# One transformer block on one core: the split of the third attention tile of each later group moves to the end of its slot

## Chip, cores and metric

The kernel runs on one core of a Trainium2 chip. A core has five engines with instruction queues of their own: TensorE (PE, matrix products), VectorE (DVE), ScalarE (ACT), GpSimd (POOL) and SyncE (SP, which here only issues DMAs). Each queue is worked off in the order in which it was written; an instruction that waits for another engine holds all that stand behind it in its own queue. The metric is the device time of one execution in microseconds (us): 510.4 us before, the median of three runs (510.28 to 510.7).

## The reference

A pre-norm transformer block on 2048 positions of width 512: attention in which each position sees itself and seven earlier positions, two apart (32 heads of width 16), and an MLP of width 1792 with a squared ReLU.

```python
def _A_ref(x, wqkv, wo):                       # H = 32, Dh = 16
    W, dil = 8, 2
    q, k, v = ...                              # of x @ wqkv
    idx = pos[:, None] - (jnp.arange(W) * dil)[None, :]
    logits = einsum("bhsd,bhswd->bhsw", q, k[idx]) * Dh ** -0.5
    attn = softmax(where(idx >= 0, logits, -1e9))
    o = einsum("bhsw,bhswd->bhsd", attn, v[idx])
    return o.reshape(B, S, D) @ wo

h  = x + _A_ref(layernorm(x), wqkv, wo)
r  = maximum(layernorm(h) @ w1 + b1, 0)
h2 = h + (r * r) @ w2 + b2
```

## The kernel before, in words

**Tiles and passes.** The positions are cut into 16 tiles of 128 (`t` = 0 to 15), four of which make a group. A first part computes q, k and v of all tiles. Then a loop over `u` = 0, 1, 2 (called the first, second and third pass below) runs the MLP of group `u` on TensorE while the tiles `4(u+1)` to `4(u+1)+3` of the next group are brought through attention, output projection and normalisation; `i` = 0 to 3 is a tile's place in its group. The last group has a loop of its own. TensorE's products are float32 made of three rounded products (high by high, low by high, high by low), so each operand is split into a high part (`hi`, ScalarE, L152) and a low part (`lo`, a subtraction on VectorE or GpSimd, L155).

**A pass.** It has 17 slots `p`. In slot `p`, TensorE gets the first MLP product of hidden block `p` (`mlp1`, L228, 12 matmuls into a bank `mm`) and the second product of block `p` - 3 (`mlp2`, L895, 12 matmuls into four banks `acc`). A bank `mm` is read out one slot later by ScalarE (`hidden`: L871, L872, then the high part `rh` at L152); its low part `rl` is a subtraction on GpSimd (L155).

**Attention** is a stream of steps that runs beside this and keeps VectorE and GpSimd busy: products of q and k (L339, `dots`; q lies in a bank `qp` that ScalarE fills, L268), their sums (L373), maximum and subtraction (L390, L392), the exponential on ScalarE (L396), the weighted values (L350, `weigh`), whose eight terms GpSimd adds up into the result tile `o` (L407, three instructions). `pump` issues as many of these steps as fit the slot by a running estimate of VectorE's and TensorE's time.

**From attention to the MLP.** A finished tile of `o` must be transposed. For the tiles 4 to 15 (`OV`) this is done by DMA in steps: `o_split` first issues attention steps until the tile is complete, then copies its two 16-bit planes apart (ScalarE, L616, `pl<-o`); `turn_dma` (SyncE, L620) transposes the planes; `o_join` two slots later joins them (ScalarE, L625), makes the high part (L152, `oh` or `ohl`) and, on VectorE, the low part (L155, `ol` or `ohl`). `wo_product` projects it (TensorE, L228, `wo`), `h_add` adds the residual and takes statistics (VectorE, L661, L163, L164, or ScalarE, L182 to L184), GpSimd turns these into a scale (L169 to L172 or L188 to L191, `rs`), `h_norm` applies it (ScalarE, L196, `hn`), and the result is transposed for the MLP by DMA (tiles in `HV`) or by TensorE (L201).

**What sets the order.** Chores are put into one of three lists for a slot: `at` (run first), `midway` and `after`. `end_slot` runs the `at` list, then the attention stream, then `midway`, then `after`:

```python
    def end_slot(pe):
        now["pe"] += pe
        run(due)
        pump()
        run(amid)
        run(late)
        now["slot"] += 1
```

The table `todo` says in which slot of a pass each step of a tile is put into which list. The third tile of a group (`i` = `RI` = 2: tiles 6, 10 and 14) has its split in slot 10 of the first two passes and slot 9 of the third. There the `at` list also holds the read-out of the bank `mm`, and the `after` list ends with the normalisation `h_norm` of an earlier tile.

Of the kernel before, what the change touches and what calls it, by code (L numbers as in the profile page):

```python
# [20 lines left out]
RI = 2  # L21
# [37 lines left out]
def block_kernel(ctx, tc, x, wqkv, wo, w1, b1, w2, b2, out):  # L59
# [53 lines left out]
    def at(delta, fn, *a):  # L113
        due.setdefault(now["slot"] + delta, []).append((fn, a))
# [7 lines left out]
# [8 lines that stand above are left out]
    def run(chores):  # L130
        todo = chores.get(now["slot"], [])
        while todo:
            fn, a = todo.pop(0)
            fn(*a)

    def dve(t):
        now["dve"] += t
# [739 lines left out]
    def mlp1(u, f):  # L877
        ps = turn["mm"].tile("mm")
        fs = slice(f * P, (f + 1) * P)
        mm3(ps, lambda k: w1_h[:, k, fs], lambda k: w1_l[:, k, fs],  # L880
            lambda k: hh[k // 2][:, k % 2], lambda k: hl[k // 2][:, k % 2])
        at(1, hidden, u, f, ps)

    def mlp2(u, f, acc, js, first=False, last=False, mid=None):

        rh, rl = hid[u, f]
        terms = [(rh, w2_h, j) for j in js] + [(rh, w2_l, j) for j in js]
        if len(js) > 1:
            terms += [(rl, w2_h, j) for j in js]
        else:  # L890
            terms.insert(1, (rl, w2_h, js[0]))
        for n, (l, w, j) in enumerate(terms):
            if mid and n == len(terms) // 2:
                mid()
            nc.tensor.matmul(acc[j], l[:, j * P:(j + 1) * P], w[f],  # L895
                             start=(first and n < len(js)),
                             stop=(last and n >= len(terms) - len(js)))
# [79 lines left out]
    for n in range(16):  # L977
        gp, t = divmod(n, 4)
# [72 lines left out]
    def load_w2(f):  # L1051
        raws[f] = row("raw2")
        nc.sync.dma_start(raws[f], w2[f * P:(f + 1) * P, :])
# [36 lines left out]
    for u in range(R - 1):  # L1090
        now["sub"] = u
        first, end = u == 0, False
        fs = list(range(FB)) if first else [*sorted(place), 12, 13]
        fs += [f for f in range(12) if f not in fs and (u < 2 or f not in ENDS)]
        fs += ENDS if u == 2 else []
        need = [] if first else [f for f in fs if f < 12 and f not in place]
        acc = [psum.tile([P, D], F32, name="acc", tag=tag) for tag in ("acc0", "acc1", "tr0", "tr1")]
        js = range(R)


        todo, halves = {}, {}
        for i in js:
            t = R * (u + 1) + i
            if not end:
                a = i // 2 if u == 2 else 0
                o0 = OP[i] - a - (2 if i >= RI and t in OV else 0)
                if t in OV:
                    turned = [(o0, at, 0, o_split, t), (o0, at if i >= RI else after, i // RI, turn_dma, ("o", t)),
                              (o0 + 2, at, 0, o_join, t)]
                else:  # L1110
                    turned = [(o0, o_T, t)]
                if t in HV:
                    h0 = 11 + i
                    turned += [(h0, midway, 0, h_split, t), (h0, after, 0, turn_dma, ("h", t)),
                               (h0 + 2, at, 0, turn_join, ("h", t))]
                for p, *what in ((LH[i] - a, at, 0, load_h, t), *turned,
                                 (WP[i] - a, wo_product, t, (0, 1, 2 + 3 * a, 3 + 3 * a))):
                    todo.setdefault(p, []).append(what)
                p, h = (HP[i], i % 2) if u < 2 else HL[i]
                if t in HV:  # L1120
                    todo.setdefault(p, []).append((at, 0, h_parts, t))
                else:
                    (todo, halves)[h].setdefault(p, []).append((h_T, t))
            todo.setdefault(UP[i], []).append((at, 0, unspill, R * u + i))
        if u == 2:
            for p, *what in ((12, at, 0, t_load, 0), (12, at, 0, t_load, 1), (13, after, 0, t_sums, 0),
                             (13, after, 0, t_sums, 1), (13, at, 1, t_split, 0),
                             (14, after, 0, t_split, 1)):
                todo.setdefault(p, []).append(what)

        def half(p):
            run(due)
            for fn, *a in halves[p]:
                fn(*a)

        for p in range(FB + LAG):
            more = 0.0
            if p == FB:
                run(due)
                dve(HOLD)  # L1140
            if u < 2 and p == FB - 2:
                dve(HOLD)
            for fn, *a in sorted(todo.get(p, []), key=lambda x: x[0] is wo_product):
                fn(*a)
                more += 2.73 if fn is wo_product else 0.0
            if p < FB:
                mlp1(u, fs[p])
                more += 2.73
                if first:
                    at(0, split_w2, p)  # L1150
                    if p + 1 < FB:
                        load_w2(p + 1)
            q = p - LAG
            if q >= 0:
                f = fs[q]
                mlp2(u, f, acc, js, q == 0, q == FB - 1,
                     (lambda: half(p)) if p in halves else None)
                more += 2.74
                if f < 12 and (need or first and p < FB - LAG):
                    free.append(place.pop(f))  # L1160
                    if need:
                        at(1, fetch, need.pop(0))
            end_slot(more)
        for i in js:
            at(u // 2, finish, R * u + i, acc[i])
# [83 lines left out]
```

## Time and profile before

| | before |
|---|---|
| median of three runs | 510.4 us |
| the profiled execution's own time | 510.82 us |
| its span, first to last instruction | 509.0 us |
| TensorE busy | 98 % of the span |
| VectorE, ScalarE, GpSimd busy | 75 %, 60 %, 70 % |
| HBM traffic over the span | 190 GB/s |
| first, second, third pass of the loop over `u` (TensorE) | about 163 to 252, 253 to 342, 343 to 430 us |

The profile is of one execution. In its rows a time is the start in us from the beginning of the span, the next number a duration in us, then come the engine, the source line, the operation, the tile written and the tile read, and a count of instructions merged into the row. A bracket at the end gives how long the engine was idle before the row and who released it. Ends of matmuls are modelled, so four matmuls are shown with a duration of 1.07 us but the next four start 0.91 us after them; only starts are compared below.

### The profile page before, as it was taken

What the parts mean: (1) busy time and instruction counts of PE and PEld (TensorE: products, weight loads), DVE (VectorE), ACT (ScalarE), POOL (GpSimd) and SP (SyncE); (2) the same over time, 40 slices, a digit from 0 to 9 for tenths busy, and PEclk for the clock granted to TensorE, in tenths of its full rate; (3) what the DMA queues carried; (4) which work ended last, traced back from release to release, by engine and by line L of the source; (5) the groups of instructions that cost most, each with busy time, mean ns of one, the idle gap of its engine ahead of it and who ended that gap; (6) DMA issues with size and microseconds to landing.
All of it is one profiled execution on the core that took longest, in us unless ns stands there. A gap on an engine that the chain in (4) does not pass through costs nothing.

```text
span 509.0 us, 7539 instructions
## 1 busy us (share of the span) xinstructions
PE 498.7 (98%) x2422; PEld 420.7 (83%) x2422; DVE 380.8 (75%) x512; ACT 304.7 (60%) x558; POOL 357.2 (70%) x434
## 2 busy tenths in 40 slices
PE   8999999999999999999999999989999999999997
PEld 7999778888888888887788888768888888998986
DVE  6469899999989799979879997898973137832233
ACT  4625677768346757386564566754556947566541
POOL 5714689986685899969777876976897465685610
PEclk9999999999999999999999999999999999999999
DMA  8577899989798898669676874967662372444212
GB/s 265 162 238 204 229 300 297 262 271 317 219 220 254 277 283 253 231 176 245 193 249 199 215 195 130 263 221 231 210 160 67 102 217 82 166 127 142 64 42 82
DMA packets 109359, 102.61 MB, mean 202 GB/s; under 512 B 29448, under 2 KB 77832, under 8 KB 109320
## 3 DMA queue, kind: packets, MB, share of 16 engines
q1 hardware_dynamic: 108376, 101.61, 68.0%
q10 hardware_dynamic: 944, 0.52, 0.3%
q8 instruction: 19, 0.31, 0.3%
q14 instruction: 20, 0.16, 0.1%
HBM read 72.65 MB, written 24.25 MB: 190 GB/s over the span
## 4 chain that ended last, share of the span: by engine, by line
PE 41%; POOL 5%; ACT 4%; DMA 3%; DVE 1%; issue 1%; SPq 0%; POOLq 0%; DVEq 0%; ACTq 0%
PE acc L895 19%; PE mm L228 12%; PE mm L818 6%; PE wo L228 3%; POOL pr L407 2%; DMA o<-pl 1%; DMA hn<-pl 1%; POOL h L674 1%; DMA h<-h_d 1%; ACT pl L625 1%; ACT pl L616 1%; ACT hn L196 1%; DVE pr L350 0%; POOL o L407 0%; PE tr L201 0%
## 5 line engine op out<-in xcount | busy, mean ns | idle before, releaser
L407 POOL TENSOR_TENSOR pr<-pr 128x512 f32<-128x512 f32 (+1 forms) x128 | 133.7, 1044 | 34.6 <-DVE pr L350 29.1
L228 PE MATMUL mm<-big_l,w_h 128*128 128x512 f32 x336 | 88.5, 390 | 1.6 <-DVE big_l L155 0.9
L350 DVE TENSOR_TENSOR pr<-ex,v 128x1024 f32<-128x1024 f32 x64 | 78.1, 1221 | 13.1 <-POOL o L407 8.1
L339 DVE TENSOR_TENSOR pr<-qp,k 128x1024 f32<-128x1024 f32 x64 | 76.8, 1200 | 8.8 <-ACT qp L268 6.9
L373 DVE TENSOR_REDUCE ex<-pr 128x64 f32<-128x1024 f32 x64 | 78.5, 1226 | 1.9
L228 PEld LDWEIGHTS mm<-big_l,w_h 128*128 128x128 f32 x336 | 62.9, 188 | 15.4 <-issue 1.3
L155 POOL TENSOR_TENSOR rl<-r,rh 128x512 fp32r<-128x512 f32 x42 | 55.5, 1322 | 20.2 <-ACT rh L152 20.2
L228 PE MATMUL mm<-big_l,xh 128*128 128x512 f32 (+1 forms) x208 | 55.8, 378 | 0.0
L228 PE MATMUL mm<-big_h,xh 128*128 128x512 f32 (+1 forms) x208 | 53.9, 380 | 1.3 <-ACT xh L152 1.0
L228 PE MATMUL mm<-big_h,xl 128*128 128x512 f32 (+1 forms) x208 | 52.7, 375 | 0.7 <-DVE xl L155 0.7
L895 PE MATMUL acc<-big_l,rh 128*128 128x512 f32 x190 | 52.2, 390 | 0.0
L895 PE MATMUL acc<-big_h,rh 128*128 128x512 f32 x190 | 52.1, 391 | 0.0
L895 PE MATMUL acc<-big_h,rl 128*128 128x512 f32 x190 | 51.7, 389 | 0.0
L228 PEld LDWEIGHTS mm<-big_h,xh 128*128 128x128 f32 x208 | 37.6, 188 | 8.9 <-ACT xh L152 2.6
L228 PE MATMUL mm<-big_l,w_l 128*128 128x512 f32 x168 | 44.9, 389 | 0.0
L228 PEld LDWEIGHTS mm<-big_h,xl 128*128 128x128 f32 x208 | 38.2, 188 | 6.9 <-DVE xl L155 1.1
L871 ACT ACTIVATE r<-mm,b_sb 128x512 f32<-128x512 f32 x42 | 28.7, 684 | 22.5 <-PE mm L228 20.7
L895 PEld LDWEIGHTS acc<-big_h,rl 128*128 128x128 f32 x190 | 35.7, 188 | 7.4
L895 PEld LDWEIGHTS acc<-big_l,rh 128*128 128x128 f32 x190 | 35.5, 188 | 7.4
L228 PEld LDWEIGHTS mm<-big_l,xh 128*128 128x128 f32 x208 | 37.5, 188 | 4.9
L895 PEld LDWEIGHTS acc<-big_h,rh 128*128 128x128 f32 x190 | 34.9, 188 | 6.7
L228 PEld LDWEIGHTS mm<-big_l,w_l 128*128 128x128 f32 x168 | 31.5, 188 | 6.6
(167 smaller groups left out, 918.7 us busy)
## 6 DMA issues: line engine op xcount, KB each, us to landing
k<-qkv_d SPq DMA_DIRECT2D x48, 288.0 KB, 3.0
v<-qkv_d SPq DMA_DIRECT2D x48, 288.0 KB, 4.1
qkv_d<-y SPq DMA_DIRECT2D x18, 512.0 KB, 4.7
big_l<-w2l_d SPq DMA_DIRECT2D x24, 256.0 KB, 3.0
xt<-in_A_x_dram SPq DMA_DIRECT2D x16, 256.0 KB, 4.2
q<-qkv_d SPq DMA_DIRECT2D x32, 128.0 KB, 3.8
h<-in_A_x_dram SPq DMA_DIRECT2D x16, 256.0 KB, 4.2
h_d<-h SPq DMA_DIRECT2D x16, 256.0 KB, 3.2
```

The source lines that it names most:

```text
L155: eng.tensor_tensor(out=dst, in0=src, in1=h, op=ALU.subtract)
L196: nc.scalar.activation(dst, src, AF.Identity, scale=rs[:, 0:1], bias=rs[:, 1:2])
L228: nc.tensor.matmul(ps, l(k), r(k), start=(n == 0), stop=(n == 3 * KB - 1))
L339: nc.vector.tensor_tensor(out=pr.rearrange("p i w h d -> p i w (h d)"), in0=qps["now"][:, j % 2].unsqueeze(2).to_broadcast([P, RI, W, GC]) ...
L350: nc.vector.tensor_tensor(out=p2, in1=vwin, op=ALU.mult, in0=e1[:, :, :, j * GH:(j + 1) * GH].unsqueeze(4).to_broadcast([P, RI, W, GH, DH]))
L373: nc.vector.tensor_reduce(out=lf[:, :, :, j * GH:(j + 1) * GH], in_=pr, axis=X, op=ALU.add)
L407: nc.gpsimd.tensor_tensor(out=dst, in0=p2[:, :, :w], in1=p2[:, :, w:2 * w], op=ALU.add)
L616: nc.scalar.copy(two_planes(planes[key][1]), halves_of(src))
L625: nc.scalar.copy(halves_of(pl).rearrange("p two n -> p n two"), two_planes(src).rearrange("p two n -> p n two"))
L818: nc.tensor.matmul(ps, sta[y][:, k], mov[x][:, k], start=(first and q == 0), stop=(last and q == len(terms) - 1), skip_group_check=True)
L871: nc.scalar.activation(r, ps, AF.Relu, bias=b1_sb[:, f:f + 1])
L895: nc.tensor.matmul(acc[j], l[:, j * P:(j + 1) * P], w[f], start=(first and n < len(js)), stop=(last and n >= len(terms) - len(js)))
```

## The change

Two entries of the table `todo` change for the third tile of each group (`i == RI`), in all three passes. The split `o_split` moves from the list that runs first in its slot (`at`) to the one that runs last (`after`). The transposing DMA `turn_dma`, which stood in the `at` list of the next slot, moves to the `after` list of the same slot, right behind the split. The joining two slots later stays. The fourth tile (`i` = 3) keeps its places, and so do the first two.

```diff
                 if t in OV:
-                    turned = [(o0, at, 0, o_split, t), (o0, at if i >= RI else after, i // RI, turn_dma, ("o", t)),
+                    turned = [(o0, after if i == RI else at, 0, o_split, t),
+                              (o0, at if i > RI else after, i // (RI + 1), turn_dma, ("o", t)),
                               (o0 + 2, at, 0, o_join, t)]
```

Since `o_split` also issues the attention steps that its tile still lacks, these move with it: they come when the slot's attention share is issued, behind the residual addition `h_add` of the slot's `at` list.

In ScalarE's queue, first pass, slot 10. `rh` and `r` are the read-out of `mm`, `big_h` the high part of a block of w2, `ex` the exponential, `hn` the normalisation of tile 4, and `pl<-o` the split of tile 6.

```order
 L872 ACTIVATE r<-r 128x512
 L152 CAST rh<-r 128x512
-L616 COPY pl<-o 128x1024
 L152 CAST big_h<-raw_2434 128x512
 L396 ACTIVATE ex<-ex 128x256
 L196 ACTIVATE hn<-h,rs 128x512
+L616 COPY pl<-o 128x1024
 L871 ACTIVATE r<-mm,b_sb 128x512
```

The split now stands behind three instructions that stood behind it.

In GpSimd's queue at the same place. The three L407 sum the last weighted values of tile 6, for which the split waits; `rl` is the low part of the read-out.

```order
 L155 TENSOR_TENSOR big_l<-raw_2359,big_h 128x512
-L407 TENSOR_TENSOR pr<-pr 128x2x256
-L407 TENSOR_TENSOR pr<-pr 128x2x128
-L407 TENSOR_TENSOR o<-pr 128x2x64
-L155 TENSOR_TENSOR rl<-r,rh 128x512
+L155 TENSOR_TENSOR rl<-r,rh 128x512
+L407 TENSOR_TENSOR pr<-pr 128x2x256
+L407 TENSOR_TENSOR pr<-pr 128x2x128
+L407 TENSOR_TENSOR o<-pr 128x2x64
 L169 TENSOR_SCALAR rs<-mv 128x1
```

The sums now come one subtraction later. On VectorE, `h_add` of tile 5 (L661, L163, L164) now stands ahead of L390 and L392; on SyncE the transposing DMA of tile 6 now stands ahead of the load of a w2 block (L1053) instead of behind it.

In ScalarE's queue, second pass, slot 10 (tile 10). `scrap` is the statistics of tile 9.

```order
 L268 COPY qp<-q 128x256
-L616 COPY pl<-o 128x1024
-L396 ACTIVATE ex<-ex 128x256
-L196 ACTIVATE hn<-h,rs 128x512
+L396 ACTIVATE ex<-ex 128x256
+L196 ACTIVATE hn<-h,rs 128x512
+L616 COPY pl<-o 128x1024
 L182 ACTIVATE scrap,nm<-h 128x512
```

Here the split falls behind two instructions; GpSimd's three sums fall behind one `rl` as in the first pass, and VectorE's `h_add` of tile 9 (L661) goes ahead of the last weighted values (L350), L390 and L392. In the third pass (tile 14) no engine's order changes.

## Prediction

> **What bounds the kernel now.** I read the page's table of engines first: TensorE is busy for all but a few us of the span.
>
> ```profile
> span 509.0 us, 7539 instructions
> PE 498.7 (98%) x2422; PEld 420.7 (83%) x2422; DVE 380.8 (75%) x512; ACT 304.7 (60%) x558; POOL 357.2 (70%) x434
> ```
>
> So a moved step is worth only what it adds to or takes from TensorE's waits. I then read TensorE's timeline over the three passes and looked for brackets.
>
> ```profile
> 231.46 1.07 PE L228 MATMUL wo<-wo_l,ohl 128*128 128x512 f32 x4
> 232.36 1.17 PE L228 MATMUL wo<-wo_h,ohl 128*128 128x512 f32 x4
> 234.22 1.20 PE L228 MATMUL mm<-big_l,w_h 128*128 128x512 f32 x4 [0.69 <-ACT r L871]
> 235.26 1.08 PE L228 MATMUL mm<-big_l,w_l 128*128 128x512 f32 x4
> ...
> 247.06 1.07 PE L895 MATMUL acc<-w_x,rl 128*128 128x512 f32 x4
> ...
> 250.81 0.66 PE L201 MATMUL tr<-ident,hn 128*128 128x128 f32 x4 [0.69 <-ACT hn L196]
> ...
> 252.69 1.07 PE L228 MATMUL mm<-big_l,w_h 128*128 128x512 f32 x4
> ```
>
> The first pass has two stalls. Four matmuls start 0.90 after the four before (231.46 to 232.36). From 232.36 the next row comes after 1.86, 0.96 too late, and the row after that 1.04 later instead of 0.91, a slower restart: 1.09 lost. From 247.06 to 252.69 are 5.63 for sixteen matmuls and eight transposes. The same sequence ends the third pass without a stall:
>
> ```profile
> 424.25 1.07 PE L895 MATMUL acc<-big_h,rl 128*128 128x512 f32 x4
> ...
> 428.82 1.07 PE L895 MATMUL acc<-big_h,rh 128*128 128x512 f32 x4
> ```
>
> That is 4.57, so the second stall costs 1.06. The second pass has three stalls, at tile 10's projection, at tile 11's, and at the start of the third pass:
>
> ```profile
> 321.39 1.20 PE L228 MATMUL wo<-wo_h,ohl 128*128 128x512 f32 x4 [0.54 <-ACT ohl L152]
> ...
> 332.25 1.20 PE L228 MATMUL wo<-wo_h,ol 128*128 128x512 f32 x4 [0.44 <-DVE ol L155]
> ...
> 343.47 1.15 PE L228 MATMUL mm<-big_l,w_h 128*128 128x512 f32 x4 [0.93 <-DVE big_l L155]
> ```
>
> Their brackets add up to 1.91. The third pass has none. All five lie behind a split of a third tile, so I went to ScalarE's timeline at those two places.
>
> **The change in the first pass (tile 6).**
>
> ```profile
> 218.44 1.05 ACT L616 COPY pl<-o 128x1024 uint16<-128x1024 uint16 x1 [7.07 <-POOL o L407]
> 219.40 0.61 ACT L152 CAST big_h<-raw 128x512 fp32r<-128x512 f32 x1
> 219.92 0.36 ACT L396 ACTIVATE ex<-ex 128x256 f32<-128x256 f32 x1
> 220.22 0.80 ACT L196 ACTIVATE hn<-h,rs 128x512 f32<-128x512 f32 x1
> 220.92 0.67 ACT L871 ACTIVATE r<-mm,b_sb 128x512 f32<-128x512 f32 x1
> ...
> 229.36 0.62 ACT L152 CAST ohl<-pl 128x512 fp32r<-128x512 f32 x1
> ...
> 230.75 1.05 ACT L616 COPY pl<-hn 128x1024 uint16<-128x1024 uint16 x1 [0.25 <-PE acc L895]
> 233.48 0.69 ACT L871 ACTIVATE r<-mm,b_sb 128x512 f32<-128x512 f32 x1 [1.69 <-POOL rl L155]
> ```
>
> ScalarE stands for 7.07 us at the split, and behind it is the exponential, for which VectorE in turn waits 3.10:
>
> ```profile
> 214.43 0.69 DVE L661 TENSOR_TENSOR h<-wo,h 128x512 f32<-128x512 f32 x1 [0.42 <-PE wo L228]
> ...
> 220.31 0.42 DVE L362 TENSOR_REDUCE sm<-ex 128x32 f32<-128x256 f32 x1 [3.10 <-ACT ex L396]
> ```
>
> No instruction is added or dropped. Step by step, in the clock of before:
>
> 1. The split gets later. GpSimd's three sums stand behind one more `rl`:
>
> ```profile
> 215.75 2.12 POOL L407 TENSOR_TENSOR pr<-pr 128x512 f32<-128x512 f32 x2
> 217.95 0.46 POOL L407 TENSOR_TENSOR o<-pr 128x128 f32<-128x128 f32 x1
> 218.37 1.29 POOL L155 TENSOR_TENSOR rl<-r,rh 128x512 fp32r<-128x512 f32 x1
> ...
> 226.57 2.11 POOL L407 TENSOR_TENSOR pr<-pr 128x512 f32<-128x512 f32 x2 [2.29 <-DVE pr L350]
> ...
> 231.67 1.78 POOL L155 TENSOR_TENSOR rl<-r,rh 128x512 fp32r<-128x512 f32 x1
> ```
>
> `rl` holds the queue for 1.26 (its duration less the 0.03 that rows overlap), so the sums end at 219.67 and the split starts at 219.70, 1.26 late.
>
> 2. The three instructions ahead of it are ready in time. The load for `big_h` was issued a slot earlier, and its row shows no wait of its own. VectorE does `h_add` first, which waits for TensorE until 214.43 either way, then statistics, maximum and subtraction: the subtraction ends near 216.85, the exponential runs to 217.2, `hn` to 218.0. They took 219.40 to 220.92, 1.52, behind the split; now they fill its wait. The read-out `r` at 220.92 therefore comes at 219.70 + 0.96 = 220.66, 0.26 earlier. ScalarE has no gap from there to 230.5, so `ohl` too is 0.26 earlier: later split, no later result.
>
> 3. VectorE restarts at 218.0 instead of 220.31. Its next sums for GpSimd come 2.3 earlier: 224.3 instead of 226.57. GpSimd runs without a gap from there through the `rl` of 231.67, which moves to about 229.4 and ends by 231.2 at the latest.
>
> 4. The first stall: TensorE waits for the read-out at 233.48, which waits 1.69 for that `rl`. Now ScalarE gets to it after 230.75 + 1.05, at 231.8, and ends it at 232.5. TensorE could go at 233.26, so the stall of 1.09 is gone with 0.8 to spare.
>
> 5. The second stall waits for tile 7's `hn`, which closes the same gapless run on GpSimd (sums, two `rs`), now 2.3 earlier as far as that queue goes, while tile 7's projection on TensorE is 1.09 earlier. Walking the queues through with these durations, tile 7's `hn` is there near 247.5 and TensorE asks near 248.7: 1.06 more, with about 1.2 to spare.
>
> SyncE's DMAs: tile 6's transpose now stands ahead of a w2 load. Both are issued only after a load of k that waits for VectorE, and VectorE is earlier, so both go out some 2 us earlier. I take nothing for them; the bounds are 0 and, if the transpose landed late, the tile 6 case among the rivals.
>
> First pass: -1.09 - 1.06 = **-2.15 us**.
>
> **The change in the second pass (tile 10).** The same delay, less compensation:
>
> ```profile
> 309.15 1.05 ACT L616 COPY pl<-o 128x1024 uint16<-128x1024 uint16 x1 [7.46 <-POOL o L407]
> 310.10 0.37 ACT L396 ACTIVATE ex<-ex 128x256 f32<-128x256 f32 x1
> 310.41 0.80 ACT L196 ACTIVATE hn<-h,rs 128x512 f32<-128x512 f32 x1
> 311.11 0.61 ACT L182 ACTIVATE scrap<-h 128x512 f32<-128x512 f32 x1
> ...
> 315.64 0.37 ACT L268 COPY qp<-q 128x256 f32<-128x256 f32 x1
> ```
>
> Only the exponential and `hn` go ahead, 311.11 - 310.10 = 1.01, against 1.26 of delay: everything behind is 0.25 later. ScalarE is gapless from 309.15 past `ohl`, so the stall at 321.39 grows by 0.25. But VectorE's gain ends here. Its product at
>
> ```profile
> 316.34 1.21 DVE L339 TENSOR_TENSOR pr<-qp,k 128x1024 f32<-128x1024 f32 x1
> ```
>
> needs the copy `qp`, which at 315.64 + 0.25 + 0.37 = 316.26 is ready just as before, so what follows from VectorE stays where it was: the loads of v that SyncE issues ahead of tile 11's transpose, that transpose, and tile 11's `ol`. TensorE comes 0.25 later to the stall at 332.25 and finds it 0.25 shorter. Bounds: +0.25 if the second stall does not give it back, and -1.9 (all three brackets) if the earlier exponential did carry through. I take **0**, since `qp` is a row that can be placed to 0.1 us.
>
> **The third pass** keeps its order, and no stall stands there: 0.
>
> **Sum.** The profiled execution took 510.82 us: 510.82 - 2.15 = 508.67. It lies 0.42 above the median of the runs; taken from the median, 510.4 - 2.15 = **508.25**, said as 508.3.
>
> **A price in step 3 that no row fixes: VectorE's and GpSimd's meetings.** The same subtraction on VectorE takes
>
> ```profile
> 222.99 1.29 POOL L155 TENSOR_TENSOR rl<-r,rh 128x512 fp32r<-128x512 f32 x1 [2.00 <-ACT rh L152]
> 223.25 1.58 DVE L155 TENSOR_TENSOR big_l<-raw,big_h 128x512 fp32r<-128x512 f32 x1
> 244.02 0.68 DVE L155 TENSOR_TENSOR w_x<-raw,w_x 128x512 fp32r<-128x512 f32 x1
> ```
>
> 1.58 when a GpSimd instruction runs beside it and 0.68 elsewhere: a meeting costs VectorE 0.90. The change moves these queues against each other by about 2 us, so meetings end and arise. The Trainium skill (SBUF — State Buffer, "SBUF: two separate sides") states that a VectorE instruction with two SBUF inputs and a GpSimd instruction exclude each other, the later one waiting for the whole of the other; the 1.58 agrees in that it ends one plain duration after the `rl` does (224.28 + 0.68 = 224.96). By that rule tile 6's low part, which I put at 229.7, meets the `rl` of step 3 and waits to about 231, for a use near 232.36: it speaks against the change but leaves the sum.
>
> **Rivals.**
>
> - *Only one of the two stalls goes.* One or two meetings of 0.90 fall on the way to tile 7's `hn` or to the `rl` of step 4, and use up the 1.2 or the 0.8 to spare. For it: GpSimd is nearly gapless there, so nothing is made good. Against: meetings also vanish. 510.4 - 1.08 = 509.3. The exclusion rule above would act in this way.
> - *The second pass gains too.* The earlier exponential gets through to tile 11 and to the start of the third pass; then up to 1.91 more: 506.4. Against it stands the row of 316.34.
> - *Slower: the split delays its own tile.* If what goes ahead of the split is not ready before it (VectorE's subtraction ends after the sums, since `h_add` waits for TensorE), the 1.26 is not filled: in the second pass `ohl` is 1.26 late and so is `qp`, tile 11 follows, and no stall gives it back; in the first pass tile 6's `ohl`, which ends at 229.98 and TensorE needs by 230.55 (231.46 less four matmuls), is 0.7 too late. 510.4 + 1.26 + 0.7 = 512.4. It decides when VectorE's subtraction ends after 218.5 (I put it at 216.85) or 309.2 (307.2).
> - *Nothing measurable.* The stalls go at their places, but TensorE, 1 to 2 us ahead, waits for the next late item: 510.4. Against: the third pass and the first half of the second show no wait at all, and GpSimd there waits for TensorE.
>
> **Chances.** Forecast 0.58 (own range 507.7 to 508.9, the 0.25 and half a stall to either side), one stall only 0.14, more 0.08, slower 0.11, nothing 0.09. A change under 0.2 % (1.0 us) can't be told from none. Faster takes the forecast, the gain in the second pass and half of the one-stall case, which lies on the border, and some of the last: 0.74; the same 0.15; slower 0.11. The range 506.8 to 510.2 holds the forecast, the one-stall case and the near part of the cases beside it.
>
> **What would show it.** Right: ScalarE's row L616 of tile 6 starts near 219.7 with the exponential near 216.9 ahead of it, VectorE's 3.10 bracket at L362 is nearly gone, no bracket of TensorE near 233 or 249; in the second pass (all 2.15 earlier) tile 10's stall is near 0.8, tile 11's near 0.2, and the one of 0.93 is still there. Wrong: the brackets of the first pass still there, or a new bracket at `wo` in either pass.

## The result, and the profile after

| | before | after |
|---|---|---|
| median | 510.4 us | 507.86 us (11 runs, beside as many of before) |
| ratio to before, 95% interval | | 0.9953 [0.9938, 0.9967] |
| the profiled execution's own time | 510.82 us | 507.5 us |
| its span | 509.0 us | 505.7 us |

The change makes the kernel 2.4 us faster (0.0047 of 510.4), between 1.7 and 3.2 us. The forecast was 508.3.

TensorE is still what bounds it. From the page of the changed kernel, the span and the busy times:

```profile
span 505.7 us, 7539 instructions
PE 497.4 (98%) x2422; PEld 421.1 (83%) x2422; DVE 382.0 (76%) x512; ACT 304.4 (60%) x558; POOL 357.2 (71%) x434
```

TensorE's timeline in the first pass, changed kernel (start, duration, engine, line, operation, out and in, count):

```profile
229.94 1.07 PE L228 MATMUL wo<-wo_h,ohl 128*128 128x512 f32 x4
...
231.75 1.07 PE L228 MATMUL wo<-wo_h,ohl 128*128 128x512 f32 x4
232.66 1.07 PE L228 MATMUL mm<-big_l,w_h 128*128 128x512 f32 x4
...
248.09 0.60 PE L201 MATMUL tr<-ident,hn 128*128 128x128 f32 x4
...
249.92 1.07 PE L228 MATMUL mm<-big_l,w_h 128*128 128x512 f32 x4
```

Both stalls are gone: `mm` starts 0.91 after the last `wo`, and no bracket stands at the transposes. Tile 6's projection starts at 229.94 instead of 230.55, 0.61 earlier. Tile 5's projection, ahead of the change's place, is already earlier by the same 0.61, and this start differs from execution to execution (see the table below). So 0.61 is added to rows of after to read them in the clock of before, that is, on the time axis of the first profile. The end of the pass, 249.92, is 2.77 ahead of 252.69. Of that 2.77 - 0.61 = 2.16 was gained in between.

TensorE's timeline in the second pass, changed kernel, tile 10's product, tile 11's, and the start of the third pass:

```profile
318.87 1.20 PE L228 MATMUL wo<-wo_h,ohl 128*128 128x512 f32 x4 [0.78 <-ACT ohl L152]
...
329.00 1.09 PE L228 MATMUL wo<-wo_h,ol 128*128 128x512 f32 x4
...
340.09 1.16 PE L228 MATMUL mm<-big_l,w_h 128*128 128x512 f32 x4 [0.88 <-DVE big_l L155]
```

Tile 10's bracket grew from 0.54 to 0.78, tile 11's (0.44) is gone, and the third (0.93) is still there. At 340.09 the kernel is 3.38 ahead of 343.47, 0.61 more than at the end of the first pass (3.38 - 2.77; that this is 0.61 again is a coincidence).

How this came about is in ScalarE's timeline, first pass, changed kernel:

```profile
216.26 0.37 ACT L396 ACTIVATE ex<-ex 128x256 f32<-128x256 f32 x1 [4.98 <-DVE ex L392]
216.54 0.81 ACT L196 ACTIVATE hn<-h,rs 128x512 f32<-128x512 f32 x1
219.08 1.05 ACT L616 COPY pl<-o 128x1024 uint16<-128x1024 uint16 x1 [1.73 <-POOL o L407]
220.03 0.69 ACT L871 ACTIVATE r<-mm,b_sb 128x512 f32<-128x512 f32 x1
...
231.09 0.68 ACT L871 ACTIVATE r<-mm,b_sb 128x512 f32<-128x512 f32 x1
...
246.66 0.81 ACT L196 ACTIVATE hn<-h,rs 128x512 f32<-128x512 f32 x1 [0.71 <-POOL rs L172]
```

The exponential runs at 216.26 instead of 219.92, `hn` behind it, and then ScalarE waits for the split, as it did before, but with less behind it. VectorE's timeline at the same place:

```profile
217.27 0.41 DVE L362 TENSOR_REDUCE sm<-ex 128x32 f32<-128x256 f32 x1
...
220.19 0.68 DVE L155 TENSOR_TENSOR big_l<-raw,big_h 128x512 fp32r<-128x512 f32 x1
...
229.15 1.21 DVE L155 TENSOR_TENSOR ohl<-pl,ohl 128x512 fp32r<-128x512 f32 x1 [0.77 <-ACT ohl L152]
```

The bracket of 3.10 at L362 is gone. GpSimd's timeline:

```profile
216.40 2.11 POOL L407 TENSOR_TENSOR pr<-pr 128x512 f32<-128x512 f32 x2
...
223.39 2.11 POOL L407 TENSOR_TENSOR pr<-pr 128x512 f32<-128x512 f32 x2
...
228.51 1.30 POOL L155 TENSOR_TENSOR rl<-r,rh 128x512 fp32r<-128x512 f32 x1
```

Its next sums start at 223.39 instead of 226.57, and the `rl` for which the first stall waited at 228.51 instead of 231.67.

### The profile page after: what moved, and what is told of

It reads as the page before. It is cut to its first block, busy times and chain, and to the rows that moved or that the text cites. A ratio compares the mean times of both kernels' runs of the same rounds, so it can differ in the third digit from the quotient of the medians.

```text
span 505.7 us, 7539 instructions
## 1 busy us (share of the span) xinstructions
PE 497.4 (98%) x2422; PEld 421.1 (83%) x2422; DVE 382.0 (76%) x512; ACT 304.4 (60%) x558; POOL 357.2 (71%) x434
## 4 chain that ended last, share of the span: by engine, by line
PE 75%; POOL 4%; DVE 3%; ACT 2%; issue 2%; DMA 1%; SPq 0%; DVEq 0%; POOLq 0%; ACTq 0%
PE mm L228 36%; PE acc L895 25%; PE wo L228 7%; PE mm L818 6%; PE tr L201 1%; DVE pr L350 1%; POOL pr L407 1%; DMA h<-h_d 1%; DVE big_l L155 1%; ACT pl L616 1%; POOL h L674 1%; DVE ex L373 0%; POOL tl L155 0%; PE half L918 0%; POOL o L407 0%
## 5 line engine op out<-in xcount | busy, mean ns | idle before, releaser
L407 POOL TENSOR_TENSOR pr<-pr 128x512 f32<-128x512 f32 (+1 forms) x128 | 134.2, 1048 | 32.3 <-DVE pr L350 26.8
L350 DVE TENSOR_TENSOR pr<-ex,v 128x1024 f32<-128x1024 f32 x64 | 78.0, 1220 | 12.9 <-POOL o L407 8.1
L339 DVE TENSOR_TENSOR pr<-qp,k 128x1024 f32<-128x1024 f32 x64 | 76.8, 1200 | 7.7 <-ACT qp L268 7.2
L373 DVE TENSOR_REDUCE ex<-pr 128x64 f32<-128x1024 f32 x64 | 78.5, 1226 | 1.9
L871 ACT ACTIVATE r<-mm,b_sb 128x512 f32<-128x512 f32 x42 | 28.7, 684 | 21.0 <-PE mm L228 20.8
```

What stands on the lines that cost most here:

```text
L339: nc.vector.tensor_tensor(out=pr.rearrange("p i w h d -> p i w (h d)"), in0=qps["now"][:, j % 2].unsqueeze(2).to_broadcast([P, RI, W, GC]) ...
L350: nc.vector.tensor_tensor(out=p2, in1=vwin, op=ALU.mult, in0=e1[:, :, :, j * GH:(j + 1) * GH].unsqueeze(4).to_broadcast([P, RI, W, GH, DH]))
L373: nc.vector.tensor_reduce(out=lf[:, :, :, j * GH:(j + 1) * GH], in_=pr, axis=X, op=ALU.add)
L407: nc.gpsimd.tensor_tensor(out=dst, in0=p2[:, :, :w], in1=p2[:, :, w:2 * w], op=ALU.add)
L871: nc.scalar.activation(r, ps, AF.Relu, bias=b1_sb[:, f:f + 1])
```

## Experiments

The table reads every profile at the same four places: the start of the first projection matmul (`wo`) of tiles 5, 8, 9 and 12. "First" is tile 8's start less tile 5's and holds both stalls of the first pass; "second" is tile 12's less tile 9's and holds the three of the second. In all of them the stretch from tile 12 to TensorE's last rows takes between 121.0 and 121.1 us except the last kernel's (121.5). The start of tile 5 is where executions differ by chance: two of the same kernel before give 211.51 and 209.21. "Landing" is the longer of the two transposing DMAs of `o` in the window 300 to 330 us, issue to landing. Ratios are to the kernel before, with 95% intervals.

| kernel | tile 5 | tile 8 | tile 9 | tile 12 | first | second | landing | ratio |
|---|---|---|---|---|---|---|---|---|
| before | 211.51 | 293.49 | 301.65 | 384.36 | 81.98 | 82.71 | 7.0 | |
| before, again | 209.21 | 291.20 | 299.36 | 381.44 | 81.99 | 82.08 | 6.5 | |
| after | 210.90 | 290.73 | 298.89 | 381.01 | 79.83 | 82.12 | 4.2 | 0.9953 [0.9938, 0.9967] |
| after, again | 211.09 | 290.93 | 299.09 | 381.23 | 79.84 | 82.14 | 4.3 | 0.9948 [0.9932, 0.9964] |
| first pass only | 210.16 | 289.99 | 298.15 | 380.85 | 79.83 | 82.70 | 6.5 | 0.9955 [0.9942, 0.9969] |
| second pass only | 210.72 | 293.18 | 301.34 | 383.54 | 82.46 | 82.20 | 4.0 | 0.9995 [0.9986, 1.0005] |
| only the DMA moved | 210.05 | 292.36 | 300.52 | 382.52 | 82.31 | 82.00 | 6.7 | 0.9998 [0.9984, 1.0011] |
| only the exponential ahead | 210.02 | 291.16 | 299.32 | 380.72 | 81.14 | 81.40 | 4.1 | 0.9949 [0.9937, 0.9961] |
| late split, early steps | 210.48 | 290.30 | 298.46 | 379.29 | 79.82 | 80.83 | 4.6 | 0.9917 [0.9904, 0.9929] |
| before, load of h early | 209.54 | 291.54 | 299.70 | 380.80 | 82.00 | 81.10 | 3.9 | 0.9969 [0.9954, 0.9984] |
| late split, early steps, h early | 211.45 | 291.27 | 299.43 | 379.58 | 79.82 | 80.15 | 3.5 | 0.9913 [0.9896, 0.9930] |
| late split, early steps, sum held | 210.80 | 290.63 | 298.79 | 378.94 | 79.83 | 80.15 | 4.6 | 0.9916 [0.9898, 0.9933] |

**Which pass gives the gain?** Two kernels make the change for one pass only; the first has `u == 0`, the second `u == 1`:

```diff
-                    turned = [(o0, at, 0, o_split, t), (o0, at if i >= RI else after, i // RI, turn_dma, ("o", t)),
+                    late_i = i == RI and u == 0
+                    turned = [(o0, after if late_i else at, 0, o_split, t),
+                              (o0, at if i >= RI and not late_i else after, int(i >= RI and not late_i),
+                               turn_dma, ("o", t)),
```

The first pass alone, expected:

> The change in the first pass alone (tile 6); tiles 10 and 14 as before. Theory (the first pass gives the predicted 2.15 us, and the rest of the gain comes from the changed order in the second pass): 510.4 - 2.2 = 508.2, ratio to before 0.9958; no TensorE bracket in the first pass, and in the second pass the brackets of before, 0.5 at tile 10 and 0.4 at tile 11. Rival (the second pass gains only because TensorE and the queues come to it 2 us ahead of the loads, whatever its own order): tile 11's bracket is gone here too, 0.4 to 0.6 us more, 507.7, ratio 0.9948, its transpose landing in about 4 us instead of 7.

The second pass alone, expected:

> The change in the second pass alone (tile 10). Theory: the first pass keeps its two stalls (1.1 each); in the second, tile 10's bracket grows by 0.25 to about 0.8, tile 11's transpose goes out sooner against the loads ahead of it, lands in about 4 us and its bracket of 0.4 is gone: in all -0.5 us, 509.9, ratio 0.999. Rival (the prediction's claim that nothing behind tile 10's product changes): tile 11's bracket only shrinks by 0.25, 0 in all, ratio 1.000. Second rival (tile 11's gain in the changed kernel came from the first pass): the bracket stays at 0.4 and tile 10's grows, +0.3, ratio 1.0005.

The first pass alone takes all of the 2.15 us of the table (81.98 to 79.83) and gives 0.9955, as good as the whole change. Its second pass is that of the kernel before, with tile 11's bracket; TensorE's timeline of that kernel:

```profile
317.88 1.20 PE L228 MATMUL wo<-wo_h,ohl 128*128 128x512 f32 x4 [0.53 <-ACT ohl L152]
...
328.75 1.19 PE L228 MATMUL wo<-wo_h,ol 128*128 128x512 f32 x4 [0.57 <-DVE ol L155]
```

So the rival that tile 11's stall goes because the first pass is over earlier falls. The second pass alone shows the brackets that its theory expected (0.79 at tile 10, none at tile 11), yet its time can't be told from no change. Its "second" of 82.20 is 0.5 less than one profile of before and 0.1 more than the other, and its "first" is 0.5 longer, with a bracket of 0.18 at tile 6's product, where VectorE's low part `ohl` just misses its time.

**Is tile 11's stall there in every execution of the kernel before?**

> The kernel before once more, for a second profile. Theory: tile 11's transpose again lands about 7 us after its issue and the brackets at tile 10 and 11 (0.5, 0.4) come again, so they belong to the order and not to one execution; rival (chance of that one execution): the transpose lands in 4 to 5 us and tile 11's bracket is absent or under 0.2.

The transpose again lands late (6.5), but without a bracket at tile 11: theory and rival are each half right. With the old order of the second pass four profiles show 7.0, 6.5, 6.5 and 6.7 us of landing, and two of the four a stall (0.44, 0.57); with the new order, 4.2, 4.3 and 4.0, and no stall in three. "Second" is 82.71, 82.08, 82.70, 82.00 with the old order, 82.37 in the mean, and 82.12, 82.14, 82.20 with the new, 82.15 in the mean. So the second pass gains about 0.2 us in the mean, not the 0.6 that the first two profiles suggest: the late landing is the order's, but whether TensorE has to wait for it differs from one execution to the next. Where the old order has no stall at tile 11 (82.08 and 82.00) the new one is about 0.1 slower, by its longer wait at tile 10; where it has one (82.71 and 82.70) the new one is about 0.55 faster. A mean of so few profiles is not clear of noise, and the second pass alone, at 0.9995, is not either.

**Was it the DMA?** Only the transposing DMA moves to the end of its slot, the split stays early:

```diff
+                    turned = [(o0, at, 0, o_split, t),
+                              (o0, at if i > RI else after, i // (RI + 1), turn_dma, ("o", t)),
```

> Only the transposing DMA of the third tiles moves, to the end of the same slot; the split and the attention steps stay early. Theory (the place of the transpose in the DMA queue is not what gives the gain): the stalls of the first pass stay at 1.1 each, ratio 0.9995 to 1.001. Rival (an earlier transpose of tiles 6 and 10, ahead of a w2 load, is a lever of its own): tile 10's bracket or a stall of the first pass shrinks, ratio 0.998 or less.

No: 0.9998, all brackets of the first pass and tile 10's as before. (Its "first" is 0.3 longer at the product with the low part of tile 6: the third group of projection matmuls starts 1.19 instead of 0.91 after the second.)

**Was it the exponential?** Only the exponential is put ahead of the split, together with the attention steps behind it on VectorE; the high part, `hn` and the DMA stay behind:

```diff
+    def ex_ahead(t):
+        pump(until=t // RI)
+        dve(next(stream) * SLOW[min(now['sub'] + 1, 2)])
...
+                    if i == RI and u < 2:
+                        turned.insert(0, (o0, at, 0, ex_ahead, t))
```

> Only the exponential is put ahead of the split in the first two passes, with the products of the next attention chunk ahead of the residual addition on VectorE; the split stays ahead of the w2 block's high part and the normalisation, the transposing DMA where it was. Theory (the 3.10 us that VectorE waits for the exponential are the lever): VectorE's bracket at the sum of the exponentials is gone or under 0.5, both stalls of the first pass are gone, ratio 0.995 to 0.997; the second pass keeps tile 10's bracket. Rival (the normalisation and the high part ahead of the split matter, or the DMA's place): at least one of the two stalls of 1.1 stays, ratio 0.998 or more.

The ratio, 0.9949, is just under the 0.995 to 0.997 that the theory expected, both stalls of the first pass are gone, and VectorE has no bracket at L362. But the first pass gains only 81.98 - 81.14 = 0.84, for a new stall came, on TensorE's timeline:

```profile
230.22 1.20 PE L228 MATMUL wo<-wo_h,ohl 128*128 128x512 f32 x4 [1.00 <-ACT ohl L152]
```

and on ScalarE's, a little earlier in the same queue (the added lines shift L871 to L875):

```profile
226.44 0.69 ACT L875 ACTIVATE r<-mm,b_sb 128x512 f32<-128x512 f32 x1 [1.84 <-POOL big_l L155]
```

The read-out waits 1.84 us until GpSimd's `big_l` has read its block of w2, and the `ohl` behind it is late by that. By the code both lie in one set of row buffers, but the attention steps that this edit moves request no such buffer, so the order of the requests is that of the kernel before. Why the read-out waits here and not there stays open. The new stall costs 81.14 - 79.83 = 1.31 of the first pass's gain.

It also brings TensorE later to the places of both old stalls, so that these are gone would not by itself show the lever. GpSimd's next sums show it:

```profile
222.49 2.13 POOL L407 TENSOR_TENSOR pr<-pr 128x512 f32<-128x512 f32 x2
```

They start 222.49 - 210.02 = 12.47 behind tile 5's projection, in the change 223.39 - 210.90 = 12.49, before 226.57 - 211.51 = 15.06. Having the exponential ahead of the split, with the steps of VectorE that this edit moves along, gives the whole lead of VectorE and GpSimd. The second pass gives more than in the change, since tile 10's bracket is only 0.27 and the last one 0.71. By the table the two stretches give 0.84 and, against the mean of the old order, 82.37 - 81.40 = 0.97, together 1.8 us; the ratio stands for 2.6 (2.0 to 3.2), and the rest is not explained.

**What do the later sums on GpSimd cost?** The change also moved tile 6's and tile 10's last attention steps behind other work. This kernel moves the split and its DMA as the change does, but leaves the steps at the head of the slot, so VectorE's and GpSimd's orders are those of before:

```diff
+                    turned = [(o0, after if i == RI else at, 0, o_split, t),
+                              (o0, at if i > RI else after, i // (RI + 1), turn_dma, ("o", t)),
                               (o0 + 2, at, 0, o_join, t)]
+                    if i == RI:
+                        turned.insert(0, (o0, at, 0, pump, t // RI))
```

> The split and its DMA late as in the change, but the attention steps that complete the tile stay at the head of the slot, so VectorE's and GpSimd's queues are as before and only ScalarE's and SyncE's orders change. Theory (the lever is the exponential ahead of the split; the later sums on GpSimd are a cost that the first pass hides and the second pays at tile 10): the split starts no later than before (218.5 in the first pass), the first pass gains 2.2, tile 10's bracket of 0.5 is gone and so is tile 11's: 507.2, ratio 0.9937, 0.5 to 0.8 us below the changed kernel. Rival (the changed order of VectorE and GpSimd, the residual addition and the read-out's low part going first, is what gives the gain): the stalls of the first pass stay, 510 or more, ratio 0.999 to 1.002.

This beats both kernels: 506.05 us, 0.9917, an interval that lies below that of the change. The first pass is as in the change (79.82), so its gain does not come from the changed order of VectorE and GpSimd, and the rival falls. The DMA moved alone gave nothing; what the change, this kernel and the one with only the exponential ahead have in common is the exponential ahead of the split. The second pass gains 82.12 - 80.83 = 1.29 more, above the 0.5 to 0.8 that were expected for the whole kernel. ScalarE's timeline of this kernel at tile 10:

```profile
302.86 0.37 ACT L396 ACTIVATE ex<-ex 128x256 f32<-128x256 f32 x1 [4.22 <-DVE ex L392]
303.37 0.82 ACT L196 ACTIVATE hn<-h,rs 128x512 f32<-128x512 f32 x1
305.99 1.05 ACT L616 COPY pl<-o 128x1024 uint16<-128x1024 uint16 x1 [1.80 <-POOL o L407]
...
316.56 0.62 ACT L152 CAST ohl<-pl 128x512 fp32r<-128x512 f32 x1
```

and of the change:

```profile
307.62 1.05 ACT L616 COPY pl<-o 128x1024 uint16<-128x1024 uint16 x1 [2.07 <-POOL o L407]
```

The split stands 7.53 behind tile 9's projection (305.99 - 298.46). In the change it is 8.73 behind (307.62 - 298.89), 1.20 later: that is the `rl` put ahead of the sums, put at 1.26. Tile 10's bracket is gone. It was worth more than its 0.78: from the four matmuls ahead of it to the row behind the projection TensorE takes 321.75 - 317.02 = 4.73 in the change and 320.22 - 316.60 = 3.62 here, 1.11 less. One bracket is left on TensorE's timeline in the three passes:

```profile
338.37 1.17 PE L228 MATMUL mm<-big_l,w_h 128*128 128x512 f32 x4 [0.72 <-DVE big_l L155]
```

**Why does the old order's transpose land late?** In the kernel before, one load moves: tile 11's block of h goes out two slots earlier.

```diff
-                for p, *what in ((LH[i] - a, at, 0, load_h, t), *turned,
+                for p, *what in ((LH[i] - a - (2 if u == 1 and i == 3 else 0), at, 0, load_h, t), *turned,
```

> The kernel before with one load moved: tile 11's block of h (256 KB) is loaded two slots earlier in the second pass, so that it is not under way just ahead of tile 11's transpose. Theory (that transpose lands after 7 us because the loads issued shortly ahead of it fill the DMA engines): it lands in 4 to 6 us, tile 11's bracket of 0.44 is gone, -0.4 us, ratio 0.999. Rival (the landing is set by when the transpose is issued, behind the loads of v that wait for VectorE): landing and bracket as before, ratio 1.000.

The transposes' line of this kernel against that of the kernel before, in the window 300 to 330 us:

```profile
DMA to landing us min/median/max: 3.9/3.9/3.9
```

```profile
DMA to landing us min/median/max: 3.8/5.4/7.0
```

Only this load moved, and the transpose goes out no earlier than before: 319.81 - 299.70 = 20.1 us behind tile 9's projection, before 320.77 - 301.65 = 19.1. So the load ahead of it is what delays it, in the one profile of this kernel. The gain is larger than expected (0.9969, 1.6 us): the stall at the start of the third pass went too. VectorE's low parts there, in the second profile of the kernel before:

```profile
335.26 3.32 DVE L155 TENSOR_TENSOR big_l<-pl,big_l 128x256 fp32r<-128x256 f32 x4
338.51 1.21 DVE L373 TENSOR_REDUCE ex<-pr 128x64 f32<-128x1024 f32 x1
339.64 1.40 DVE L155 TENSOR_TENSOR big_l<-tr,big_l 128x256 fp32r<-128x256 f32 x4
```

and with the early load:

```profile
335.46 2.52 DVE L155 TENSOR_TENSOR big_l<-pl,big_l 128x256 fp32r<-128x256 f32 x4
```

The first four low parts take 0.80 less. In the kernel before GpSimd's sums start beside them (335.43), here a little later (336.22). The kernel below that has the early load as well repeats this (2.52 at 334.20, the sums at 334.96). That the meeting is the cause was not tried by itself.

**Does the last stall go?** Three kernels on one chip: the change again, the late split with early steps and the early load of h, and the late split with early steps and an added charge to VectorE's estimated time (`dve(1.2)`) that holds back VectorE's sum (L373 above) until the last low parts are done:

```diff
             if u < 2 and p == FB - 2:
                 dve(HOLD)
+            if p == FB + 1 and u == 1:
+                dve(1.2)
```

The change again:

> The changed kernel again, on the same chip as the next two, for a direct comparison and a second profile. Theory (the second pass with the changed order is as in the first profile): ratio 0.993 to 0.997; tile 11's transpose lands in about 4 us, no bracket at tile 11, 0.8 at tile 10, 0.9 at the start of the third pass. Rival (that landing was chance): it lands in 6 us or more, or tile 11's bracket is there.

With the load early:

> The late split with early attention steps, and tile 11's block of h loaded two slots earlier as well. Theory (the early load shortens the meeting at the start of the third pass, as it did alone, 0.9 us): that stall of 0.7 shrinks or goes, ratio 0.990 to 0.991. Rival (with the earlier split tile 11's transpose already lands in 4.6 us, and the stall hangs on VectorE's order alone): as the kernel without the early load, 0.9915 to 0.992.

With the sum held back:

> The late split with early attention steps, and the sum of products that VectorE does ahead of the last low parts of the second pass (1.1 us) put behind them. Theory (TensorE's stall of 0.7 to 0.9 at the start of the third pass is that sum standing ahead of the low parts): the bracket is gone, ratio 0.990 to 0.991, no new one in the third pass. Rival (the low parts wait for something else, or the attention work pushed behind comes late in the third pass): bracket stays or a new one comes, ratio 0.9915 or more.

The change repeats itself (0.9948, brackets of 0.79 and 0.88, landing 4.3). Both others lose the last stall ("second" 80.15, 0.68 less than 80.83). With the sum held back a small one comes in the third pass, where the read-out is late:

```profile
390.13 1.20 PE L228 MATMUL mm<-big_l,w_h 128*128 128x512 f32 x4 [0.15 <-ACT r L871]
```

It starts 1.22 instead of 0.91 after the row ahead, and the stretch behind tile 12 is 0.4 to 0.5 longer (121.5). So with the early load the last stall goes and no other comes, while with the sum held back theory and rival are each half right. The ratios, 0.9913 and 0.9916, can't be told from the 0.9917 without these edits; the change stands at 0.9948 beside them.

## Why the prediction was right, and where it was not

**Step 1, the split 1.26 later:** right. It starts at 219.08, in the clock of before 219.69, where 219.70 was put.

**Step 2, the read-out 0.26 earlier:** right. `r` at 220.03 is 220.64 there; 220.66 was put.

**Step 3, VectorE at 218.0, sums at 224.3:** right, 217.27 + 0.61 = 217.88 and 223.39 + 0.61 = 224.00. The kernels with early steps and with only the exponential ahead show that the earlier exponential is what gives this lead.

**Step 4, the first stall gone with 0.8 to spare:** right. The read-out ends at 231.09 + 0.68 = 231.77, and TensorE asks at 232.66, 0.89 later.

**Step 5, the second stall gone with about 1.2 to spare:** gone, but the room was half of that. Tile 7's `hn` ends at 246.66 + 0.81 = 247.47 and TensorE asks at 248.09: 0.62. In the clock of before `hn` is there at 248.08, not near 247.5. The row of before shows where that number fails:

```profile
249.94 0.81 ACT L196 ACTIVATE hn<-h,rs 128x512 f32<-128x512 f32 x1 [0.71 <-POOL rs L172]
```

It ends at 250.75. The 2.3 us that the step names would bring this to 248.45, with only 0.25 to spare, so 247.5 does not follow from the lead that it gives; the queue came 249.94 - (246.66 + 0.61) = 2.67 earlier. With 2.3 alone the room would have been a quarter of a us, so that the stall went clear of it is in part luck: another meeting of 0.90 would have brought some of it back.

**Meetings:** as put, but for one. Tile 6's low part starts at 229.15 (229.76 in the clock of before, put at 229.7), beside the `rl` of 228.51, and takes 1.21. It ends at 230.97 there ("about 231"). By the exclusion rule of the Trainium skill (SBUF — State Buffer, "SBUF: two separate sides") it should end one plain duration behind the `rl`, 229.81 + 0.68 = 230.49; the trace has 230.36. The prediction's own example is off by the same 0.13: it ends at 223.25 + 1.58 = 224.83, not at 224.96. The `big_l` that took 1.58 beside an `rl` takes 0.68 now that none runs there. But it meets a small instruction of GpSimd, and here GpSimd's is the longer one, 0.81 us where the same row of before takes 0.26 (it ends at 220.92, the `big_l` at 220.19 + 0.68 = 220.87):

```profile
220.11 0.81 POOL L172 TENSOR_SCALAR rs<-mv,rs 128x1 f32<-128x1 f32 x1
```

So the price of that meeting shrank and went over to GpSimd. The prediction put meetings as a cost of VectorE alone.

**SyncE's DMAs, taken at nothing:** tile 6's transpose went out at 220.72 instead of 224.25, and the kernel with only the DMA moved shows no gain from its place.

**First pass, -2.15:** measured -2.16 in the first profile and -2.15 with the first pass alone. The whole forecast, 2.1 us less, lies within the measured 1.7 to 3.2.

**Second pass, 0:** tile 10's bracket came as put (0.78 for 0.8) and the third stayed (0.88). The part on tile 11 was wrong: "the loads of v that SyncE issues ahead of tile 11's transpose, that transpose, and tile 11's `ol`" did not stay where they were. The step stopped VectorE's gain at L339, which waits for `qp`, and there it does stop. But what SyncE issues ahead of that point had already moved. SyncE's timeline before (start, time to issue):

```profile
313.55 0.32 SPq L247 DMA_DIRECT2D k<-qkv_d  x1
315.20 0.32 SPq L247 DMA_DIRECT2D v<-qkv_d  x1
315.57 1.25 SPq L620 DMA_TRANSPOSE o<-pl  x1
...
317.50 0.42 SPq L590 DMA_DIRECT2D h<-in_A_x_dram  x1
...
320.77 3.46 SPq L620 DMA_TRANSPOSE o<-pl  x1
```

and after:

```profile
308.50 0.32 SPq L247 DMA_DIRECT2D k<-qkv_d  x1
310.15 0.32 SPq L247 DMA_DIRECT2D v<-qkv_d  x1
310.52 1.25 SPq L620 DMA_TRANSPOSE o<-pl  x1
...
312.46 0.42 SPq L590 DMA_DIRECT2D h<-in_A_x_dram  x1
...
317.75 2.17 SPq L620 DMA_TRANSPOSE o<-pl  x1
```

VectorE's timeline after shows what released them and where its gain ended:

```profile
307.31 1.16 DVE L339 TENSOR_TENSOR pr<-qp,k 128x1024 f32<-128x1024 f32 x1
...
308.90 1.22 DVE L350 TENSOR_TENSOR pr<-ex,v 128x1024 f32<-128x1024 f32 x1
...
313.52 1.23 DVE L339 TENSOR_TENSOR pr<-qp,k 128x1024 f32<-128x1024 f32 x1 [2.14 <-ACT qp L268]
```

The loads of k and v go out as these two products end (308.47 and 310.12). Everything from there through the block of h goes out 5.0 earlier than before, tile 11's transpose only 3.0 (2.8 of either is the lead from the first pass and the start). So the block of h is issued 5.3 us ahead of that transpose instead of 3.3 (317.75 - 312.46 and 320.77 - 317.50), and the transpose lands in 4.2 instead of 7.0. Over seven profiles this is worth the 0.2 us above: the term was off in its mechanism more than in its size. That the size came out near 0 is luck, for a loss of about 0.1 without the old stall at tile 11 and a gain of about 0.55 with it happen to lie on either side.

**Rivals.** "Only one of the two stalls goes" and "nothing measurable" did not come about, nor did the split delay its own tile: the subtraction was done by 216.26, which is 216.87 in the clock of before, well ahead of the 218.5 that it named. But the price that it names is real: tile 10's split comes 1.20 later than in the kernel with early steps, which gains 1.29 us more in the second pass. "The second pass gains too" came about in a small part, and not through tile 11's exponential but through the loads.

## What to carry to other kernels

Where an in-order queue stands at a wait, look at what is behind the waiting instruction and who needs it: here one exponential of 0.37 us, held by a copy that waited for another engine, cost TensorE 2.15 us in the first pass, in two stalls 14 and 31 us behind it. When an entry of a schedule is moved, look at what it drags along: the split took its attention steps with it, and leaving these where they were was worth another 1.3 us. A DMA queue whose loads wait for compute moves with that compute, so a step can change the landing of a transfer that it does not touch.

## What was not expected of the hardware

In the twelve profiles, tile 11's transposing DMA, one 128x1024 block of 16-bit values, landed after 3.5 to 4.6 us where the load of 256 KB ahead of it was issued 4.5 us or more earlier or was moved away, and after 6.5 to 7.0 us where that load was issued 3.3 to 3.6 us earlier; its issue on SyncE's queue then took 3.0 to 3.5 us instead of 1.3 to 2.5.

The executions of one kernel differ mostly before tile 4: its first projection starts at 203.35 and 201.05 in the two profiles of before, and from there to tile 8 they agree within 0.01 us (90.14 and 90.15).
